# Sliding-window attention and squared-ReLU MLP, two layers on one core: LayerNorm transposes by DMA, and attention logits that arrive already spread over the partitions

## The chip, the cores and the metric

The kernel runs on one core of a Trainium2 chip. The metric is the device time of one execution in microseconds (us), median of several. The 13 executions of the kernel before lie within 0.15% (1329.62 to 1331.54 us).

The engines are called by their names in the profile: PE is TensorE (matrix multiply), PEld its weight loads, DVE is VectorE, ACT is ScalarE, POOL is GpSimd, SP is the engine that issues DMAs. An engine's queue, below, is the list of its instructions in the order in which the compiled program has them.

## The reference, cut to what matters

Two layers of attention and two MLPs, 2048 tokens, width 1024, inner width 3584, bfloat16:

```python
x = x + A(layernorm(x));  x = x + B(layernorm(x))      # twice, same weights

# A: 32 heads of 32; token s looks at s, s-2, ... s-14 (W = 8, dilation 2)
logits = einsum("bhsd,bhswd->bhsw", q, kg) * Dh ** -0.5
attn   = softmax(where(idx >= 0, logits, -1e9));  o = einsum("bhsw,bhswd->bhsd", attn, vg)
return o @ wo
# B
h = relu(x @ w1 + b1) ** 2;  return h @ w2 + b2
```

## The kernel before

A block is 512 tokens; there are four blocks to a layer, so eight in all, numbered 0 to 7. PE's program for block u is, in this order: the query and key projections of block u+1 (128 matmuls of 128x512), the output projection of block u (64, `py<-wt,oT`), the value projection of block u+1 (64, `pq`), the MLP of block u (224 up, `ph`; 224 down, `py<-wt,r2t`). Attention on DVE and LayerNorm on ACT are woven in beside it by a scheduler that estimates when each input is ready.

LayerNorm of a tile of 128 tokens, then eight PE transposes into PSUM and a copy out:

```python
def ln_transpose(self, xt, xnT, tl, dve_stats=False, evac_act=False):
    if dve_stats:   # bn_stats, bn_aggr on DVE; Ln, Exp on ACT; nmr on DVE
        ...
    else:           # two passes of ACT over the tile (sum, then square), then five small ones
        nc.scalar.activation(out=xn[:], in_=xt, func=ACTF.Identity, accum_out=s1[:])
        ...
        nc.scalar.activation(out=xn[:], in_=xt, func=ACTF.Square, bias=nmean[:], scale=1.0, accum_out=s2[:])
        ...
    nc.scalar.activation(out=xn[:], in_=xt, func=ACTF.Identity, bias=nmr[:], scale=rstd[:])
    pt = self.ps_t.tile([128, self.KD, 128], BF, name="pt", tag="pt")
    for kd in range(self.KD):
        nc.tensor.transpose(pt[:, kd, :], xn[:, kd * 128:(kd + 1) * 128], self.ident[:])
    with self.tc.high_priority():
        ...         # copy to xnT on VectorE, in three blocks on ScalarE
```

Attention of a half block (256 tokens, `hb`): for each of eight chunks c, DVE makes the product P of q with eight shifted views of k. In blocks 1 to 7 a tree adds the eight P in fours; PE sums over the channels of a head with small matmuls (`lg`, 32 columns). In block 0 (`STREAM`) there is no tree: PE adds all eight. Softmax follows, with tokens on the partitions; then the probabilities are copied four times (`p4`) and transposed back on PE (`ptp`):

```python
    # prod:  P = q * shifted k;  STREAM: stream_red(d, P) on PE;  else two levels of the tree
    # red:   for w in range(W): for i, Pp in enumerate(d["finals"]):
    nc.tensor.matmul(lg[:, tl2, w, :], Pp[:, w, tl2 * 128:(tl2 + 1) * 128], self.ind[:], ...)
    # sm:    max, subtract, Exp      p4f: sum, reciprocal, p4 = z * l
    # tr:
    nc.tensor.transpose(ptp[:, w, :], p4[:, tl2, w].rearrange("p h r -> p (h r)"), self.ident[:])
    nc.scalar.copy(pb[:, :, tl2 * 128:(tl2 + 1) * 128], ptp[:])
    # av:    pr = pb * shifted v, three adds -> oT
```

## Time and profile before

| | before |
|---|---|
| time, median of 4 | 1330.51 us (1329.84 to 1330.92) |
| span of the profiled execution | 1328.1 us |
| PE / DVE / ACT busy | 97% / 62% / 51% |
| 128x512 matmuls | 5632, starts 216 ns apart |
| distance from one block's MLP to the next, blocks 2 to 6 | 161.1 us |

From the groups of instructions of the kernel before, by shape. Columns: line, engine, operation, output<-inputs, shape, count | busy us, mean ns of one | idle time of the engine in front of them and what ended it:

```profile
L485 PE MATMUL ph<-xnT,wt 128*128 128x512 bf16 x1792 | 395.1, 380 | 0.8 <-DVE xnT L198 0.8
...
L335 DVE TENSOR_TENSOR P<-P 128x2048 bf16<-128x2048 bf16 x84 | 102.3, 1219 | 0.4
...
L193 PE MATMUL pt<-ident,xn 128*128 128x128 bf16 x512 | 41.5, 227 | 29.3 <-ACT xn L190 28.6
...
L398 PE MATMUL ptp<-ident,p 128*128 128x128 bf16 x256 | 17.1, 219 | 0.6 <-DVE p L386 0.5
...
L362 PE MATMUL lg<-ind,P 128*128 128x32 bf16 x448 | 13.7, 177 | 0.7 <-DVE P L335 0.7
...
L349 PE MATMUL lg<-ind,P 128*128 128x32 bf16 x256 | 8.9, 177 | 0.1
```

A PE instruction lasts longer than the distance to the next (380 ns against 216 for `ph`, 227 against 56 for `pt`; they overlap), so costs are counted by the distance of starts: 216 ns for 512 columns, 56 ns for a transpose in a stream of eight between matmuls, 25 ns for a 32-column logit matmul, all at a granted clock of 1.00. The group of LayerNorm transposes (`pt`) also carries PE's largest wait, 28.6 us for `xn` of ACT.

The timeline of PE in block 2 of the kernel before (start us, us, what, count, [idle before it <- what ended it]) shows how those waits lie:

```profile
426.95 9.66 PE L457 MATMUL py<-wt,oT 128*128 128x512 bf16 x44
437.51 0.62 PE L193 MATMUL pt<-ident,xn 128*128 128x128 bf16 x8 [0.90 <-ACT xn L190]
437.97 4.48 PE L457 MATMUL py<-wt,oT 128*128 128x512 bf16 x20
...
443.12 0.62 PE L193 MATMUL pt<-ident,xn 128*128 128x128 bf16 x8 [0.24 <-ACT xn L190]
443.58 5.79 PE L268 MATMUL pq<-xnT,wt 128*128 128x512 bf16 x26
449.55 0.62 PE L193 MATMUL pt<-ident,xn 128*128 128x128 bf16 x8 [0.19 <-ACT xn L190]
```

### The profile page before, as it was taken

What the parts mean: (1) busy time and instruction counts of PE and PEld (TensorE: products, weight loads), DVE (VectorE), ACT (ScalarE), POOL (GpSimd) and SP (SyncE); (2) the same over time, 40 slices, a digit from 0 to 9 for tenths busy, and PEclk for the clock granted to TensorE, in tenths of its full rate; (3) what the DMA queues carried; (4) which work ended last, traced back from release to release, by engine and by line L of the source; (5) the groups of instructions that cost most, each with busy time, mean ns of one, the idle gap of its engine ahead of it and who ended that gap; (6) DMA issues with size and microseconds to landing.
All of it is one profiled execution on the core that took longest, in us unless ns stands there. A gap on an engine that the chain in (4) does not pass through costs nothing.

```text
span 1328.1 us, 17393 instructions
## 1 busy us (share of the span) xinstructions
PE 1292.2 (97%) x7104; PEld 679.8 (51%) x7104; DVE 830.0 (62%) x1170; ACT 681.1 (51%) x1229; POOL 2.9 (0%) x9
## 2 busy tenths in 40 slices
PE   6999999999999999999999999999999999998998
PEld 3665444654446544455445554455544555443443
DVE  4599993394934949268582777719676197926011
ACT  4647826287342964239561494615836166142622
POOL 0000000000000000000000000000000000000000
PEclk9999999999999999999999999999999999999999
DMA  8434544546355554656457464456644564346341
GB/s 214 160 127 158 175 138 151 203 160 203 124 197 185 180 175 143 199 189 207 122 176 233 161 221 151 137 188 211 202 127 163 193 216 137 122 151 225 127 135 56
DMA packets 180847, 223.69 MB, mean 168 GB/s; under 512 B 8608, under 2 KB 143776, under 8 KB 180768
## 3 DMA queue, kind: packets, MB, share of 16 engines
q1 hardware_dynamic: 177168, 222.58, 51.1%
q0 software_dynamic: 3600, 0.01, 0.4%
q8 instruction: 55, 0.90, 0.3%
q14 instruction: 24, 0.20, 0.0%
HBM read 209.98 MB, written 12.58 MB: 168 GB/s over the span
## 4 chain that ended last, share of the span: by engine, by line
PE 73%; DVE 14%; ACT 11%; issue 1%; DMA 0%; SPq 0%; ACTq 0%
PE py L506 29%; PE ph L485 28%; PE pq L268 12%; DVE P L316 5%; DVE P L335 4%; ACT xn L190 3%; ACT xn L181 3%; ACT xn L185 2%; PE pt L193 1%; DVE pr L411 1%; PE py L457 1%; PE ptp L398 1%; DVE xm L459 1%; ACT vT L270 1%; PE lg L362 1%
## 5 line engine op out<-in xcount | busy, mean ns | idle before, releaser
L485 PE MATMUL ph<-xnT,wt 128*128 128x512 bf16 x1792 | 395.1, 380 | 0.8 <-DVE xnT L198 0.8
L506 PE MATMUL py<-wt,r2t 128*128 128x512 bf16 x1792 | 392.6, 379 | 0.0
L268 PE MATMUL pq<-xnT,wt 128*128 128x512 bf16 x1536 | 344.5, 381 | 0.8 <-DVE xnT L198 0.8
L506 PEld LDWEIGHTS <-r2t 128*128 128x128 bf16 x1792 | 174.5, 98 | 207.1 <-ACT r2t L490 0.4
L485 PEld LDWEIGHTS <-wt 128*128 128x128 bf16 x1792 | 174.2, 98 | 206.5 <-issue 2.9
L268 PEld LDWEIGHTS <-wt 128*128 128x128 bf16 x1536 | 216.7, 144 | 107.0 <-issue 3.0
L489 ACT ACTIVATE r<-ph,b1T 128x512 bf16<-128x512 f32 x224 | 152.9, 683 | 98.2 <-PE ph L485 97.2
L411 DVE TENSOR_TENSOR pr<-pb,vT 128x2048 bf16<-128x2048 bf16 x128 | 155.1, 1226 | 44.2 <-ACT pb L399 44.2
L316 DVE TENSOR_TENSOR P<-qT,kT 128x2048 bf16<-128x2048 bf16 x128 | 153.5, 1224 | 36.6 <-ACT qT L270 36.5
L490 ACT ACTIVATE r2t<-r 128x512 bf16<-128x512 bf16 x224 | 140.6, 629 | 5.5
L270 ACT CAST kT<-pq 128x512 bf16<-128x512 f32 x64 | 37.6, 587 | 188.9 <-PE pq L268 188.9
L457 PE MATMUL py<-wt,oT 128*128 128x512 bf16 x512 | 115.1, 383 | 0.0
L335 DVE TENSOR_TENSOR P<-P 128x2048 bf16<-128x2048 bf16 x84 | 102.3, 1219 | 0.4
L412 DVE TENSOR_TENSOR pr<-pr 128x1024 bf16<-128x1024 bf16 x128 | 86.3, 688 | 0.0
L516 DVE TENSOR_TENSOR xo<-py,xm 128x512 bf16<-128x512 f32 x32 | 22.1, 692 | 101.9 <-PE py L506 101.9
L399 ACT COPY pb<-ptp 128x1024 bf16<-128x1024 bf16 x32 | 31.6, 1013 | 104.1 <-PE ptp L398 103.9
L457 PEld LDWEIGHTS <-oT 128*128 128x128 bf16 x512 | 50.0, 99 | 59.1 <-issue 2.0
L512 DVE TENSOR_TENSOR xm<-py,xm 128x512 f32<-128x512 f32 x64 | 44.0, 687 | 52.0 <-PE py L506 52.0
L270 ACT CAST qT<-pq 128x512 bf16<-128x512 f32 x64 | 37.5, 586 | 65.3 <-PE pq L268 65.3
L193 PE MATMUL pt<-ident,xn 128*128 128x128 bf16 x512 | 41.5, 227 | 29.3 <-ACT xn L190 28.6
L521 DVE TENSOR_TENSOR xof<-py,xm 128x512 f32<-128x512 f32 x32 | 22.1, 692 | 76.4 <-PE py L506 56.5
L193 PEld LDWEIGHTS <-xn 128*128 128x128 bf16 x512 | 32.4, 101 | 51.6 <-ACT xn L190 45.7
(61 smaller groups left out, 734.2 us busy)
## 6 DMA issues: line engine op xcount, KB each, us to landing
wt<-in_B_w_dram SPq DMA_DIRECT2D x88, 1024.0 KB, 6.1
wt<-in_A_wqkv_dram SPq DMA_DIRECT2D x48, 1024.0 KB, 6.3
wt<-in_B_w_dram SPq DMA_DIRECT2D x32, 768.0 KB, 4.6
wt<-in_A_wo_dram SPq DMA_DIRECT2D x16, 1024.0 KB, 6.2
xt<-xs SPq DMA_DIRECT2D x32, 512.0 KB, 4.5
xt<-in_A_x_dram SPq DMA_DIRECT2D x32, 256.0 KB, 3.6
xs<-xof SPq DMA_DIRECT2D x32, 256.0 KB, 3.0
out_dram<-xo SPq DMA_DIRECT2D x32, 128.0 KB, 2.0
```

The costliest lines, as they stand in the source:

```text
L193: nc.tensor.transpose(pt[:, kd, :], xn[:, kd * 128:(kd + 1) * 128], self.ident[:])
L268: nc.tensor.matmul(pq[:], fetch(nm)[kd // 4][:, kd % 4, c0:D:8], xnT[:, kd, :], start=(kd == 0), stop=(kd == KD - 1))
L270: nc.scalar.copy(dst[:, c0, off:off + BLK], pq[:])
L316: pi = nc.vector.tensor_tensor(P[:], qT[:, c, None, hb * HB:(hb + 1) * HB].to_broadcast([128, W, HB]), _win_ap(kT[:, c, :], HALO + hb * HB ...
L335: nc.vector.tensor_tensor(other[:], other[:], cur[:], ALU.add)
L411: nc.vector.tensor_tensor(pr[:], pb[:], vwin, ALU.mult)
L412: nc.vector.tensor_tensor(pr[:, 0:4, :], pr[:, 0:4, :], pr[:, 4:8, :], ALU.add)
L457: nc.tensor.matmul(py[:], oT[:, c, tl * 128:(tl + 1) * 128], wos[db][:, c, :], start=(c == 0), stop=(c == NCH - 1))
L485: nc.tensor.matmul(ph[:], wt[:, kd, cc * 128:(cc + 1) * 128], xnT[:, kd, :], start=(kd == 0), stop=(kd == KD - 1))
L489: nc.scalar.activation(out=r[:], in_=ph[:], func=ACTF.Relu, bias=self.b1T[:, f_idx:f_idx + 1], scale=1.0)
L490: nc.scalar.activation(out=r2t[:], in_=r[:], func=ACTF.Square)
L506: nc.tensor.matmul(py[:], r2[kf][:, tl * 128:(tl + 1) * 128], w2s[gi][:, j, :], start=(kf == 0), stop=(kf == KFH - 1))
```

## The change

Its intent: to take work off PE. (1) LayerNorm tiles are transposed by DMA from SBUF to SBUF, except in block 0's first LayerNorm, the last block's second, and the fourth tile of each second LayerNorm. (2) One 128x128 group matrix sums the channels of a head and spreads the result over the head's partitions in one step, so logits come out in the layout in which they are needed; no transposing back, no maximum. (3) The tree on DVE goes all the way, in block 0 too. (4) float16 in attention. The core of the diff:

```diff
-        self.ind = const.tile([128, H], BF, name="ind")
+        self.grp = const.tile([128, H, 4], F16, name="grp")      # 1 where both channels are of one head
+        self.mask01 = const.tile([128, W, HALO], F32, name="mask01")
...
-        xn = self.xp.tile([128, D], BF, name="xn", tag="xn")
+        xn = self.xp.tile([128, D], BF, name="xn", tag="xn", bufs=4)
...
+        if scr is not None:
+            with self.tc.high_priority():
+                nc.sync.dma_start_transpose(xnT[:, tl], xn[:])
+            return
...
-        xnT = self.act.tile([128, self.KD, BLK], BF, name="xnT", tag="xnT")
+        xnT = self.act.tile([128, 4, self.KD, 128], BF, name="xnT", tag="xnT")
...
-                if STREAM: ... stream_red(d, P)
-                while lvl in d["levels"] and lvl < MAXL:
+                while lvl in levels:
                     nc.vector.tensor_tensor(other[:], other[:], cur[:], ALU.add)
...
         def red(hb):
+            for j in range(W // 2):
+                lg = self.ps_lg.tile([128, 2, HB], F32, name="lg", tag="lg")
+                nc.tensor.matmul(lg[:], self.grp[:].rearrange("p h r -> p (h r)"), P[:, 2 * j:2 * j + 2, :], start=True, stop=True)
+                nc.scalar.activation(out=e[:, 2 * j:2 * j + 2, :], in_=lg[:], func=ACTF.Exp, scale=self.scale)
-        def sm / p4f / tr
+        def norm(hb):        # mask, three adds over w, reciprocal, pb = e * ri
...
-            self.ln_transpose(xm[:], xnT, tl, dve_stats=(u == self.n_layers * self.NB - 1), evac_act=(u == 0))
+            last = u == self.n_layers * self.NB - 1
+            self.ln_transpose(xm[:], xnT, tl, dve_stats=last,
+                              scr=None if last or tl == 3 else self.xnd[...])    # only whether it is None counts
```

392 of 512 LayerNorm transposes leave PE for 49 DMA transposes, 120 stay; 256 probability transposes vanish; 704 small logit matmuls become 64 of 512 columns.

## The prediction

> **What bounds it now.** TensorE. The page: PE 97% busy, VectorE 62%, ScalarE 51%, DMA half. There are 5632 matmuls of 128x512; in the trace one starts 216 ns after the other (the timeline has 80 in 17.28 us). [...] That is 1216.5 us of the 1328.1 us span. The other 111.6 us: start to the first projection 17.2; tail 3.6; 512 LayerNorm transposes at 56 ns (28.7); 256 probability transposes at 56 ns (14.3); 704 small logit matmuls at 25 ns (17.6); waits of PE for LayerNorm in the last unit about 7.5; the rest: cold start, and waits of 0.6 to 1.3 us at LayerNorm transposes for xn. One block takes 161.1 us in the steady part (the chain's projection stretches start that far apart).
>
> **What the change does.**
> 1. 392 of 512 LayerNorm transposes become 49 DMA transposes (256 KB each); -22 us on PE, and most of the waits for xn before them, about -6.
> 2. Probability transposes vanish: -14. 704 logit matmuls become 64 of 512 columns: 13.8 against 17.6, -4. All on the critical engine.
> 3. VectorE: the tree gets 28 more full adds (1.14 us apart in the timeline), 112 for 84; 37 xnT copies (0.69 us) go; softmax in the wide layout costs an estimated 6.4 us a half block (f32 adds 2.0; reciprocal of 256, from 549 ns for 64, 2.2; 2048-wide f32 product 2.2) against about 5.5. ScalarE loses the 32 copies of 1013 ns and 12 of 1008, and gets 48 more exps.
>
> In the steady blocks VectorE has room (about 85 of 150 us for attention), so the PE savings count: an estimated 155 to 156 us a block.
>
> **The loss.** In block 0 PE has only projections to do before it needs attention, 320 matmuls. Its logits were streamed on PE without a tree; now VectorE must do 14 tree adds (16 us). In the trace its last attention product of block 0 ends near 114 us and PE finishes the output projection at 120. After, I count from the last q at 48: products and adds to 72, normalise 78, first half 97, normalise and four residual adds 106, second half 124; PE, ready near 90, waits about 25 us in the output projection and ends it near 131, 11 us later than now. The rest after that: 1208.2 us now, an estimated 1169 then.
>
> **DMA transposes.** A 256 KB load lands in 3.6 us here. [...] The third tile's has 7 to 8 us before the MLP's first matmul. Mostly hidden.
>
> **Prediction:** 1302 us (-2.1%), 8 in 10 between 1284 and 1325. Faster by over 2%: 0.50; within 2%: 0.43; slower by over 2%: 0.07.
>
> **What would show it.** Starts of the chain's projection stretches 155 to 156 us apart. PE waiting on VectorE's oT about 25 us in the first output projection, and nowhere else. Adds x112, no ptp group, lg x64 at 216 ns. [...] little PE wait on DMA.
>
> **What would make it wrong.** Transposes that land in 10 us or more, or hold up weight loads behind them on the one queue: a stall in every block. Strided xnT reads over 216 ns. A smaller wait in block 0 (then about 1285).

The sum: 11 us more in block 0 and 39 us less in the rest, 1302 us. Its 2.0 and 2.2 us for f32 adds and product lie near what DVE takes for f32 in the kernel before, 1218 ns for 1024 columns, 687 for 512 and 428 for 256. What it calls cold start is a slower pace at the start of that trace: eight transposes take 1.03 us at 10.4 us and 0.62 us at 35.9 us, at a granted clock of 1.00 both times; the cause isn't shown.

## More of the kernel before

From the page of the kernel before, the span, part 1 (busy us, share of the span, instructions) and part 2's line for ACT (tenths busy in 40 slices):

```profile
span 1328.1 us, 17393 instructions
PE 1292.2 (97%) x7104; PEld 679.8 (51%) x7104; DVE 830.0 (62%) x1170; ACT 681.1 (51%) x1229; POOL 2.9 (0%) x9
...
ACT  4647826287342964239561494615836166142622
```

PE is the engine to relieve.

## The result, and the profile after

| | before | after | predicted |
|---|---|---|---|
| time, median | 1330.53 us (13 runs) | 1307.4 us (8 runs) | 1302, 1284 to 1325 |
| ratio | | 0.9827 [0.9817, 0.9836] | 0.979 |
| block 0's output projection ends | 119.9 us | 124.6 us | 131 us |
| the rest of the span | 1208.2 us | 1181.0 us | 1169 us |
| distance from one block's MLP to the next, blocks 2 to 6 | 161.1 us | 155.7 to 157.8 us | 155 to 156 us |

Ratios are the mean time of one kernel's runs over that of the other's of the same rounds, so not quite the ratio of the quoted medians. Executions over 1.5% slower than the fastest of the same kernel are left out of the means.

From the page of the changed kernel, the same lines:

```profile
span 1305.6 us, 14886 instructions
PE 1255.2 (96%) x5816; PEld 636.3 (49%) x5816; DVE 856.6 (66%) x1143; ACT 655.8 (50%) x1233; POOL 3.4 (0%) x9
...
ACT  4734934279142892239731495415934167142622
```

The groups of the changed kernel that answer to those above, in the same columns:

```profile
L323 DVE TENSOR_TENSOR P<-P 128x2048 f16<-128x2048 f16 x112 | 136.2, 1220 | 1.1
...
L397 PE MATMUL py<-wt,oT 128*128 128x512 bf16 x512 | 118.1, 391 | 11.4 <-DVE oT L364 11.4
...
L348 DVE RECIPROCAL ri<-dn 128x256 f32<-128x256 f32 x16 | 28.0, 1749 | 0.2
...
L335 PE MATMUL lg<-P,grp 128*128 128x512 f16 x64 | 17.3, 390 | 2.5 <-DVE P L323 2.5
...
L196 PE MATMUL pt<-ident,xn 128*128 128x128 bf16 x120 | 11.6, 254 | 29.7 <-ACT xn L189 29.6
```

The counts are the ones that the diff promises: 112 tree adds of the same 1220 ns, 64 logit matmuls, no `ptp` group, 120 `pt`. But look at the last column of the last line. There are 392 fewer transposes on PE, and PE still waits 29.6 us at them for `xn` of ACT, where it waited 28.6 us before. The work went, the wait stayed. (Without the start of the kernel and the last block, where the change takes nothing from the waits, the idle time at `pt` is 11.3 us before and 12.4 us after.)

The DMA transposes themselves are quick. From the changed kernel's list of DMA issues (what, queue, count, median us from issue to landing):

```profile
xnT<-xn SPq DMA_TRANSPOSE x49, 3.3
```

They land in 2.7 to 6.5 us, and one, 256 KB, holds SP 1.23 us in the median (1.63 at most). Packets under 512 B rose from 8608 to 60352 with the 49 transposes, (60352 - 8608) / 49 = 1056 for each.

Two places of the changed kernel's PE timeline show the cost and the wait. Block 0, its output projection, which begins at 93.2 us:

```profile
93.21 1.67 PE L397 MATMUL py<-wt,oT 128*128 128x512 bf16 x7
96.01 5.57 PE L397 MATMUL py<-wt,oT 128*128 128x512 bf16 x25 [1.13 <-DVE oT L364]
108.96 3.60 PE L397 MATMUL py<-wt,oT 128*128 128x512 bf16 x8 [7.38 <-DVE oT L364]
113.52 3.59 PE L397 MATMUL py<-wt,oT 128*128 128x512 bf16 x8 [0.96 <-DVE oT L364]
...
122.64 1.90 PE L397 MATMUL py<-wt,oT 128*128 128x512 bf16 x8 [0.96 <-DVE oT L364]
124.58 11.81 PE L273 MATMUL pq<-xnT,wt 128*128 128x512 bf16 x54
```

PE waits here for DVE. From 93.0 to 124.6 us DVE is busy 31.60 of 31.60 us, so only less work on DVE in front of it, or another order of that work, can shorten it. The 64 matmuls would take 13.8 us at 216 ns; they take 31.4 us: 11.4 us of waits, and 20 us for the matmuls, which run at a granted clock of 0.73 in the mean of this stretch. (The clock is 1.00 up to 104.6 us, 0.50 from there, 3 us into the wait of 7.4 us, to 121.7 us, and 1.00 after that; the next pair of `oT` chunks comes 4.6 us after the one before, and the eight matmuls for a pair take 3.6 us even so, so here the slow clock hides behind DVE.)

Block 2, the stretch that stands for the steady blocks:

```profile
424.39 13.98 PE L397 MATMUL py<-wt,oT 128*128 128x512 bf16 x64
438.20 11.82 PE L273 MATMUL pq<-xnT,wt 128*128 128x512 bf16 x54
451.93 0.62 PE L196 MATMUL pt<-ident,xn 128*128 128x128 bf16 x8 [1.91 <-ACT xn L189]
452.39 2.33 PE L273 MATMUL pq<-xnT,wt 128*128 128x512 bf16 x10
454.56 1.89 PE L427 MATMUL ph<-xnT,wt 128*128 128x512 bf16 x8
```

Before, four tiles of transposes lay here, each behind a wait of 0.1 to 0.9 us. Now one tile is left, the fourth, and it alone waits 1.9 us. The output projection runs without a break (64 matmuls in one group). Counted from its start, PE gets to the fourth tile at 25.6 us (26.0 before), but ACT ends that tile's `xn` only at 27.5 us (26.1 before).

How busy is ACT there? The table of stretches gives, for a stretch, its length, the busy us (and instructions) of PE, PEld, DVE, ACT and POOL, the granted clock, the DMA share and GB/s. Taken from the first LayerNorm pass of block 2's output projection to a place 2 to 6 us into the MLP's first down-projection (cut where that begins, ACT's shares below are the same within 4 points); before, then after:

```profile
432.60:490.50 57.90, 56.45 (x352) 30.07 (x351) 39.57 (x45) 52.10 (x98) 0.00 (x0) 1.00 0.55 181
```

```profile
430.00:486.60 56.60, 54.55 (x259) 27.56 (x258) 53.34 (x68) 56.03 (x116) 0.00 (x0) 1.00 0.78 220
```

ACT is busy 52.10 of 57.90 us before (90%), and 56.03 of 56.60 us after (99%). In the rest of the same period it is busy 26.68 of 94.30 us. So ACT, 50% busy over the span, has almost no slack for a third of this block, which stands for the steady ones, and that is the third in which PE needs LayerNorm from it. The busiest engine differs within one period: in this stretch it is ACT (56.03 us against PE's 54.55), in the rest PE (94.30 of 94.30 us).

This gives the theory that the experiments test: **PE's removed work pays in full, but PE's waits are set by ACT's load between the output projection and the middle of the MLP's first half, and removing PE work doesn't shorten them.** Rivals: the wait belongs to the place of the fourth tile's transposes in PE's order; it belongs to the fourth tile being on PE at all; or the loss is all in block 0, in the DVE tree.

### The profile page after: what moved, and what is told of

It is laid out like the page before. It is cut to its first block, busy times and chain, and to the rows that moved or that the text cites. A ratio compares the mean times of both kernels' runs of the same rounds, so it can differ in the third digit from the quotient of the medians.

```text
span 1305.6 us, 14886 instructions
## 1 busy us (share of the span) xinstructions
PE 1255.2 (96%) x5816; PEld 636.3 (49%) x5816; DVE 856.6 (66%) x1143; ACT 655.8 (50%) x1233; POOL 3.4 (0%) x9
## 2 busy tenths in 40 slices
DMA packets 232582, 236.39 MB, mean 181 GB/s; under 512 B 60352, under 2 KB 195520, under 8 KB 232512
## 4 chain that ended last, share of the span: by engine, by line
PE 60%; ACT 19%; DVE 16%; issue 2%; DMA 2%; SPq 0%; ACTq 0%
PE py L448 29%; PE ph L427 21%; PE pq L273 9%; DVE P L314 6%; DVE P L323 4%; ACT xn L184 4%; ACT xn L180 3%; ACT r L431 3%; ACT r2t L432 3%; ACT xn L189 3%; DVE xm L399 1%; DVE pr L361 1%; ACT vT L275 1%; DMA xt<-in_A_x_dram 1%; DVE xm L405 1%
## 5 line engine op out<-in xcount | busy, mean ns | idle before, releaser
L273 PE MATMUL pq<-xnT,wt 128*128 128x512 bf16 x1536 | 339.2, 382 | 0.8 <-DVE xnT L201 0.8
L427 PEld LDWEIGHTS <-wt 128*128 128x128 bf16 x1792 | 175.9, 98 | 213.8 <-issue 4.3
L273 PEld LDWEIGHTS <-wt 128*128 128x128 bf16 x1536 | 220.2, 144 | 114.9 <-issue 5.0
L314 DVE TENSOR_TENSOR P<-qT,kT 128x2048 f16<-128x2048 f16 x128 | 154.0, 1224 | 30.1 <-ACT qT L275 30.0
L361 DVE TENSOR_TENSOR pr<-pb,vT 128x2048 f16<-128x2048 f16 x128 | 153.0, 1224 | 0.3
L323 DVE TENSOR_TENSOR P<-P 128x2048 f16<-128x2048 f16 x112 | 136.2, 1220 | 1.1
L275 ACT CAST kT<-pq 128x512 f16<-128x512 f32 x64 | 37.5, 587 | 191.7 <-PE pq L273 188.3
L397 PE MATMUL py<-wt,oT 128*128 128x512 bf16 x512 | 118.1, 391 | 11.4 <-DVE oT L364 11.4
L362 DVE TENSOR_TENSOR pr<-pr 128x1024 f16<-128x1024 f16 x128 | 84.3, 685 | 0.0
L275 ACT CAST qT<-pq 128x512 f16<-128x512 f32 x64 | 37.4, 584 | 64.5 <-PE pq L273 64.5
L336 ACT ACTIVATE e<-lg 128x512 f32<-128x512 f32 x64 | 34.7, 606 | 50.7 <-PE lg L335 49.5
L180 ACT ACTIVATE xn<-xm 128x1024 bf16<-128x1024 f32 x28 | 29.3, 1048 | 50.9 <-DVE xm L399 50.9
```

Source lines behind the costliest of these rows:

```text
L273: nc.tensor.matmul(pq[:], fetch(nm)[kd // 4][:, kd % 4, c0:D:8], xnT[:, :, kd, :], start=(kd == 0), stop=(kd == KD - 1))
L275: nc.scalar.copy(dst[:, c0, off:off + BLK], pq[:])
L314: pi = nc.vector.tensor_tensor(cur[:], qT[:, c, None, hb * HB:(hb + 1) * HB].to_broadcast([128, W, HB]), _win_ap(kT[:, c, :], HALO + hb * ...
L323: nc.vector.tensor_tensor(other[:], other[:], cur[:], ALU.add)
L361: nc.vector.tensor_tensor(pr[:], pb[:], vwin, ALU.mult)
L362: nc.vector.tensor_tensor(pr[:, 0:4, :], pr[:, 0:4, :], pr[:, 4:8, :], ALU.add)
```

## The experiments

Eleven further kernels ran, one of them twice (e7, e7b); all gave correct results. Each was compared with the kernel before on the same chip; "us" is the median of the fast runs. The expectations speak of theories by letter; the numbers beside them tell what each would have meant. "Waits per block" below are worked out from the trace: the distance from each PE matmul's start to the next, less 216, 56 or 25 ns for the kind, summed from the start of block 2's MLP to that of block 6's where it exceeds 60 ns, divided by four. Some traces lack 50 to 65 matmul records; a gap of a whole 216 ns, which a missing record or a granted clock of 0.50 leaves (eight matmuls take 3.60 us at it in block 0 of the changed kernel, 1.90 us at 1.00), isn't counted. "Period" is the distance from the start of one block's MLP to the next one's; the range has all six, but where the first is given apart.

| kernel | us | ratio to before [95%] | period, us | waits per block, us |
|---|---|---|---|---|
| before | 1330.5 | 1 | 161.1; first 163.0 | 2.1 |
| after | 1307.4 | 0.9827 [0.9817, 0.9836] | 155.7 to 157.8; first 159.4 | 2.7 |
| e1_pe_ln | 1325.4 | 0.9961 [0.9946, 0.9976] | 159.4 to 160.3 | 2.1 |
| e2_dma_ln_only | 1327.0 | 0.9984 [0.9966, 1.0002] | 158.3 to 160.3; first 165.9 | 3.4 |
| e3_stream0 | 1307.9 | 0.9835 [0.9819, 0.9851] | 156.5 to 160.6 | 2.9 |
| e4_stats3 | 1320.9 | 0.9920 [0.9905, 0.9935] | 156.2 to 159.0 | 3.0 |
| e7_tl3_dma | 1305.2 | 0.9815 [0.9799, 0.9832] | (one profile, e7b) 154.1 to 160.5 | 2.6 |
| e8_bf16 | 1306.8 | 0.9825 [0.9810, 0.9839] | like after | 2.6 |
| e9b_late_stats | 1322.3 | 0.9932 [0.9916, 0.9947] | 156.5 to 159.7 | 3.5 |
| e10_all | 1315.6 | 0.9886 [0.9871, 0.9901] | 156.6 to 158.4 | 3.2 |
| e11_mid | 1304.3 | 0.9810 [0.9794, 0.9825] | 154.6 to 157.7 | 2.6 |
| e14_mid_sa | 1293.1 | 0.9720 [0.9707, 0.9734] | 154.1 to 156.9 | 0.1 |
| e15_mid_sa_stream | 1290.9 | 0.9704 [0.9691, 0.9717] | 154.1 to 157.3 | 0.1 |

### e1_pe_ln: the attention half of the change alone

All LayerNorm transposes back on PE, the rest as in the changed kernel:

```diff
-                              scr=None if u == 0 else self.xnd[...])
+                              scr=None)
...
-                              scr=None if last or tl == 3 else self.xnd[...])
+                              scr=None)
```

> The changed kernel with all LayerNorm transposes back on TensorE; the attention rewrite stays. Theory A (a TensorE transpose costs its 56 ns on the engine that bounds, and the wait of 2.3 us a block for the last LayerNorm tile comes from ScalarE's chain and has nothing to do with DMA): 392 transposes come back, of which 64 fall into block 0's wait, so about +18 us: 1326 us, and the waits for xn are still 2 to 3 us a block. Rival B (the DMA transposes cause the wait for LayerNorm, by latency or by holding up the queue): the waits shrink to well under 1 us a block, about -12 us against A: 1314 us or less.

Measured: 1325.4 us, on theory A's 1326. Five us less than before; block 0's MLP starts 6.7 us later (141.9 against 135.2 us), the first period is 2.7 us shorter, and each later one 0.8 to 1.7 us. Waits per block are what they were before, 2.1 us, with no DMA transpose at all, so rival B is out. ACT's share of the stretch is 98% here.

### e2_dma_ln_only: the DMA transposes alone

The kernel before, with the DMA transposes in the same places as the changed kernel, the same layout of `xnT`, and four `xn` buffers:

```diff
+        if dma:
+            with self.tc.high_priority():
+                nc.sync.dma_start_transpose(xnT[:, tl], xn[:])
+            return
...
-            self.ln_transpose(xt, xnT, tl, dve_stats=(u == 0), evac_act=(1 <= u <= 2))
+            self.ln_transpose(xt, xnT, tl, dve_stats=(u == 0), dma=(u > 0))
...
+                              dma=(u < last and tl < 3))           # second LayerNorm (written short)
```

> The kernel before with one part of the change alone: LayerNorm transposes by DMA as in the changed kernel, the old attention (streamed block 0, two-level tree, probability transposes) stays. Theory A: 392 transposes of 56 ns leave TensorE, about -22 us, the wait for the last tile stays: 1306 to 1310 us, so nearly all of the whole change's 23 us. The attention rewrite would then be worth about nothing in sum (about -15 us in the steady blocks, against a longer wait in block 0). Rival (the attention rewrite carries the gain, DMA transposes are given back in waits): 1318 us or more.

Measured: 1327.0 us, where 1306 to 1310 was expected. This is the largest miss. 56 transposes a block went (7 tiles of 8, 3.1 us at 56 ns), yet the waits rose from 2.1 to 3.4 us a block, so a steady period is only about 2 us shorter (161.1 - 3.14 + 1.27 = 159.2; 158.3 to 160.3 measured). The stretch in question, of this kernel:

```profile
435.90:495.50 59.60, 57.37 (x339) 30.19 (x339) 39.20 (x44) 57.64 (x116) 0.00 (x0) 1.00 0.76 223
```

ACT is busy 57.64 of 59.60 us: here ACT keeps its copies of `ptp` besides the LayerNorm, and its delay shows at the fourth tile, and later at the MLP's `r2t`. In addition the first period grew, 165.9 us against 163.0. The trace shows where: PE waits 2.3 and 0.5 us at `ptp` (166.7 and 167.9 us) for DVE's `p`, behind a DVE that had itself waited 2.4 us for ACT's exponentials (162.7 us), and 3.4 us at `pt` (299.7 us) for ACT's `xn`; after the waits at `ptp` PE is slower too: four 128x512 matmuls from 168.7 us take 1.91 us, where four take 1.03 us at a granted clock of 1.00 (e11). ACT is busy 12.94 of the 13.00 us from 155 to 168 us, so this is ACT's load once more. The four `xn` buffers weren't tried alone.

So -5.3 (e1, ratio 0.9961) and -3.6 us alone (e2, by the medians; its interval reaches 1, so it isn't clear of noise), but -23 us together. The two halves don't add. By the traces the together is better by about 4 us before block 0's MLP, 4 in the first period, 5 in the next five and 1 in the tail. A reason, argued and not tested: each half leaves ACT the load that the other removes or spreads, or leaves PE work that hides the waits.

### e7_tl3_dma and e7b_tl3_dma: the fourth tile by DMA too

```diff
-                              scr=None if last or tl == 3 else self.xnd[...])
+                              scr=None if last else self.xnd[...])
```

> The changed kernel with the fourth tile's LayerNorm transpose on DMA as well (seven more). Theory A: the tile is ready at the same time from ScalarE, then needs 1.2 us of issue and 3.3 us to land instead of 0.5 us on TensorE and a copy of 0.7 us, so the wait moves from before the transposes to before the MLP's first matmul and grows: 0.5 to 1.5 us a block, 1311 to 1318 us. Rival (latency of the DMA is hidden, the last tile needs no exception): 1304 us, by the 56 transposes saved.

Measured: 1305.2 us in three runs (1304.4 to 1308.3), the same as the changed kernel; 1311 to 1318 was expected. A fourth execution took 1904.4 us at a granted clock of 0.656, whose cause no run tells (with it the median is 1306.8), and the profile fell there.

> The fourth tile's transpose by DMA once more, for a profile at full clock (the one of the earlier run fell in a stretch at a granted clock of 0.656). Its time was that of the changed kernel within the interval. If the wait only moved: about 2 to 2.5 us a block in front of the MLP's first matmul, none at transposes, and the period 156 to 157 us.

Measured: 1307.9 us in the one run (state unknown, clock 0.986). PE's timeline in block 2:

```profile
440.76 13.98 PE L273 MATMUL pq<-xnT,wt 128*128 128x512 bf16 x64
457.44 1.89 PE L427 MATMUL ph<-xnT,wt 128*128 128x512 bf16 x8 [2.27 <-DMA xnT<-xn]
```

The value projection now runs unbroken, and the wait has moved to the MLP's first matmul: 2.3 us for the DMA transpose of the last tile. That rules out the rival that the fourth tile loses because it is on PE. ACT ends `xn` 27.5 us after the output projection's start, as in the changed kernel. That alone would be no wait here: it is 0.7 us before PE is free. The 2.3 us come of ACT's late `xn` and the 3.0 us to landing together.

### e8_bf16: bfloat16 in place of float16

```diff
-F16 = mybir.dt.float16
+F16 = mybir.dt.bfloat16
```

> The changed kernel with bfloat16 in the attention tensors in place of float16. If the data type does not matter for time (both have 2 bytes): 1307 us, VectorE products still 1.22 us. The error against the reference should be larger. Rival: the float16 products or the float16 logit matmul run at another pace, then the mean of these groups differs by over 5%.

Measured: 1306.8 us, periods as in the changed kernel, correct. float16 neither costs nor gains time; the tree adds take 1218 ns here against 1220 in the changed kernel. The record has no error figure, so the expectation of a larger error stays unchecked.

### e3_stream0: block 0's logits streamed on PE again

```diff
+                if u == 0:       # no tree: PE sums the eight chunks into four open groups
+                    for j in range(W // 2):
+                        nc.tensor.matmul(lgs[j][:], grp, cur[:, 2 * j:2 * j + 2, :],
+                                         start=(c == 0), stop=(c == NCH - 1))
+                    continue
...
-            e = self.att.tile([128, W, HB], F32, name="e", tag="e")
+            e = self.att.tile([128, W, HB], F32, name="e", tag="e", bufs=2)
```

> The changed kernel, but block 0 adds its eight products up on TensorE (64 logit matmuls for 8) with no tree on VectorE, as the kernel before did in its own layout; a second buffer for the exponentials. Theory A (the wait of TensorE in the first output projection, about 17 us in all, is VectorE's queue of work, of which the 14 tree adds are 16 us): VectorE ends block 0's attention near 113 us instead of 122.7, TensorE has 12 us more to do but in time that it waited: the first output projection ends near 115 us instead of 124.5, total about -9 us: 1298 us. Rival (the wait has another cause, or TensorE's added 12 us count in full): 1307 to 1319 us.

Measured: 1307.9 us, the same as the changed kernel. Block 0's output projection ends at 121.2 us instead of 124.6, and its MLP starts 2.6 us earlier (136.8 against 139.4). An arithmetic slip of the expectation: with PE at work until 105.0 us and 64 matmuls to come (13.8 us), 119 us was the least possible. The gain is gone later: the next period is 160.6 us against 159.4, and those after it up to 158.4. The second `e` buffer is a confound. So the tree in block 0 costs 2.6 to 3.4 us there, and while ACT limits the blocks after it, taking it back is worth nothing.

### e4_stats3: the fourth tile's statistics on DVE

```diff
-            self.ln_transpose(xm[:], xnT, tl, dve_stats=last,
+            self.ln_transpose(xm[:], xnT, tl, dve_stats=last or tl == 3,
```

> The changed kernel with the statistics of the fourth tile's LayerNorm taken on VectorE (bn_stats) instead of two passes on ScalarE. Theory C (the wait for the last tile depends on how long ScalarE's chain is): ready about 2.5 us earlier, the wait of 2.3 us a block vanishes, about -14 us: 1294 us. Theory D (it depends on where the schedule puts the eight transposes in TensorE's queue: here they move up from behind 54 to behind 38 matmuls of the projection in most blocks, 3.5 us earlier, because the scheduler also believes in the earlier xn): a wait of 1.5 to 3 us a block remains: 1304 to 1309 us.

Measured: 1320.9 us, 13.5 us worse than the changed kernel. PE, in block 0:

```profile
124.36 13.97 PE L273 MATMUL pq<-xnT,wt 128*128 128x512 bf16 x64
148.18 1.03 PE L196 MATMUL pt<-ident,xn 128*128 128x128 bf16 x8 [9.85 <-ACT xn L189]
```

In block 0 DVE is the engine with the backlog. The two statistics instructions stood in its queue behind attention and ran at 141.95 and 143.67 us; PE waited 9.9 us, and block 0's MLP began at 151.1 us, 11.7 us later. In the steady blocks the waits stayed at 3.0 us and split between the transposes (7.3 us in four blocks) and the MLP's `r2t` (4.7 us). In block 2 `xn` is finished 3.7 us sooner (23.8 us after the output projection's start, against 27.5), but the compiled order has the transposes sooner too, behind 38 matmuls of the value projection and not 54, and PE waits 1.7 us. That is what theory D said of the steady blocks; the loss in block 0 it didn't foresee. Moving one tile's statistics away from ACT isn't enough, and in block 0 it goes to the wrong engine.

### e9b_late_stats: the same, with the transposes after the value projection

```diff
+        if late:
+            return finish            # the eight PE transposes and the copy, to be called later
...
+            if nm == "wv" and c0 == NCH - 1 and u > 0:
+                self.late_pt()
```

> As the run before (statistics of the fourth tile on VectorE), and the eight transposes are put later in the program, so that they stand behind 56 or 64 matmuls of the projection. Theory D: xn is there when TensorE reaches them, the wait is under 0.5 us a block (at most 1 us before the MLP where they stand at the very end): about -13 us, 1294 us. If a wait of 2 us stays at the transposes or reappears in front of the MLP's first matmul for another reason (a DMA transpose of tiles 0 to 2 not landed): 1304 to 1308 us.

Measured: 1322.3 us. Block 0 lost as in e4 (MLP at 150.5 us). In block 2 the wait moved again. PE, then DVE, of the same stretch:

```profile
461.08 0.61 PE L197 MATMUL pt<-ident,xn 128*128 128x128 bf16 x8
461.53 1.90 PE L276 MATMUL pq<-xnT,wt 128*128 128x512 bf16 x8
465.23 1.89 PE L430 MATMUL ph<-xnT,wt 128*128 128x512 bf16 x8 [1.80 <-ACT nmr L188]
```

```profile
461.03 1.22 DVE L326 TENSOR_TENSOR P<-P 128x2048 f16<-128x2048 f16 x1
462.17 2.36 DVE L317 TENSOR_TENSOR P<-qT,kT 128x2048 f16<-128x2048 f16 x2
464.44 0.68 DVE L199 COPY xnT<-pt 128x1024 bf16<-128x1024 bf16 x1
```

The transposes no longer wait, but their copy out of PSUM stands behind three wide attention instructions on DVE and ends at 465.1 us; the MLP's first matmul starts 0.1 us after it. The profile names "ACT nmr" as what ended that wait, but the fourth tile's `nmr` had been done at 457.7 us, before the transposes ran: the name printed isn't what ended this wait, it was the copy. So this wait, 2.0 us a block, ends on DVE in every block (0.1 us after the copy); another 1.5 us a block stands at ACT's `r2t`.

### e10_all: e3 and e9b together

> Both mends together: block 0 streamed, fourth tile's statistics on VectorE and its transposes late. If the two waits are independent the gains add: -9 and -13 us, 1285 us (3.4% below the kernel before). If they share a cause or one gives back what the other takes: 1294 us or more.

Measured: 1315.6 us, with block 0's MLP at 147.1 us and periods of 156.6 to 158.4 us. Streaming relieves DVE in block 0 and gives back 6.8 us of what e9b lost (by the medians; 3.4 us of it before block 0's MLP), but against the changed kernel nothing was gained in the steady blocks.

### e11_mid: the transposes in the middle of the value projection, DVE statistics not in block 0

```diff
-            if nm == "wv" and c0 == NCH - 1 and u > 0:
+            if nm == "wv" and c0 == 6 and u > 0:
...
-            self.late_pt = self.ln_transpose(xm[:], xnT, tl, dve_stats=last or tl == 3, ...)
+            self.late_pt = self.ln_transpose(xm[:], xnT, tl, dve_stats=last or (tl == 3 and u > 0), ...)
```

> The changed kernel with the fourth tile's statistics on VectorE in blocks 1 to 7 only (not in block 0, where VectorE is behind with attention), and its transposes behind 48 of the 64 value-projection matmuls. Read from the two runs before: xn is ready about 23.8 us after the output projection begins, TensorE comes to the transposes at 24.2 us, and the copy out of PSUM has 3.4 us until the MLP needs it. Theory E (the 2 us a block are a race of three places: ScalarE's chain, the place of the transposes in TensorE's queue, and VectorE's queue in front of the copy): the wait before the MLP falls below 0.5 us a block, the period from 156.5 to about 154.8 us, the total by about 11 us: 1296 us; block 0's MLP starts at 139 us as in the changed kernel. Rival (there is a floor of about 2 us a block whose place alone moves, as in the two runs before): 1305 to 1309 us.

Measured: 1304.3 us. This is the run that kills the rival of place. PE hardly waits at the fourth tile in the steady blocks, or before the MLP (0.5 us in four blocks). It waits 2.6 us a block all the same (9.9 us in four blocks at `r2t`), in the middle of the MLP:

```profile
478.52 3.19 PE L451 MATMUL py<-wt,r2t 128*128 128x512 bf16 x14
482.93 0.39 PE L451 MATMUL py<-wt,r2t 128*128 128x512 bf16 x1 [1.22 <-ACT r2t L435]
484.17 2.12 PE L451 MATMUL py<-wt,r2t 128*128 128x512 bf16 x9 [0.85 <-ACT r2t L435]
```

`r2t` is the square of the squared ReLU, made by ACT. ACT in that stretch is at 54.19 of 56.40 us (96%). Its queue is behind, and PE pays the delay where it first needs what ACT has not made yet.

### e14_mid_sa: less LayerNorm on ACT

e11, and the statistics of the first LayerNorm also on DVE, in all blocks but block 1 (before, in block 0 alone):

```diff
-            self.ln_transpose(xt, xnT, tl, dve_stats=(u == 0),
+            self.ln_transpose(xt, xnT, tl, dve_stats=(u != 1),
```

> As the run before, and the first LayerNorm's statistics (tiles of blocks 2 to 7) on VectorE too, 24 tiles. Theory F (the waits of up to 1.2 us for r2t at the first down-projection matmuls are ScalarE's backlog, which two LayerNorm passes a tile add to): these waits vanish, 0.3 to 0.6 us a block: 2 to 4 us under the run before. Rival (VectorE now holds the chain up, as it did in block 0 with the statistics there): equal or slower.

Measured: 1293.1 us, 11.2 us below e11 by one flag; 2 to 4 us was expected, too little, since e11's `r2t` wait alone was 2.5 us a block. The stretch, of e11 and of this kernel:

```profile
427.60:484.00 56.40, 54.50 (x258) 27.55 (x256) 54.63 (x72) 54.19 (x110) 0.00 (x0) 1.00 0.75 221
```

```profile
427.10:482.00 54.90, 54.90 (x262) 28.01 (x261) 54.38 (x75) 42.98 (x80) 0.00 (x0) 1.00 0.79 228
```

ACT fell from 54.19 to 42.98 us (96% to 78%), and PE from 54.50 busy of 56.40 us to 54.90 of 54.90: no idle. The place where e11 waited runs through in this kernel:

```profile
478.09 5.13 PE L451 MATMUL py<-wt,r2t 128*128 128x512 bf16 x23
```

Waits are 0.12 us a block, and four periods in a row are 154.1 us. PE's own work in a block of the changed kernel is 704 x 0.216 + 8 x 0.216 + 8 x 0.056 = 154.2 us, so nothing is left to take but work. DVE took the statistics without harm: 54.38 us busy in the stretch against e11's 54.63. That also answers the rival that DVE, just as full in this stretch, makes PE wait: at 99% of it (54.38 of 54.90 us) PE doesn't wait at all.

### e15_mid_sa_stream: with block 0 streamed

e14 and e3's streaming.

> As the run before, with block 0 streamed. In the earlier run streaming alone started block 0's MLP 2.6 us earlier and gave it back later. If the blocks after it are no longer held by ScalarE, the 2.6 us stay: 2 to 3 us under the run before. If not, no difference.

Measured: 1290.9 us, the fastest kernel: 39.6 us below before and 16.5 us below the changed kernel. Block 0's MLP starts 3.6 us earlier than in e14 (135.0 against 138.6), and 2.2 us of that reach the end by the medians (the runs of the two overlap, 1289.2 to 1292.7 against 1292.3 to 1293.9, so the size is not firm). The same streaming gained nothing in e3, where ACT set the pace of the later blocks.

## Why the prediction was right, and where it was wrong

**Right: PE bounds the kernel, and its removed work pays.** A steady period by PE's own work: before, 704 x 0.216 + 64 x 0.056 (LayerNorm) + 32 x 0.056 (`ptp`) + 64 x 0.025 (logits) = 159.0 us, and 2.1 us of waits, which makes 161.1 (161.1 measured). After, 154.2 and 2.7 us of waits, which makes 156.9 (157.0 measured in the mean of the same four periods). The DMA transposes landed in 3.3 us in the median, 2.7 to 6.5, and matmuls that read `xnT` in the new layout still start 216 ns apart (120 `ph` in 26.06 us in block 2).

**Right in kind, mis-sized: the loss in block 0.** The step "and ends it near 131, 11 us later than now" was 124.6 us, 4.7 us later. PE was ready at 93.2 us ("near 90") and DVE was the limit, as said. But "waits about 25 us" was 17.6 us over the matmuls' own 13.8: 11.4 us of waits and some 6 us of slower clock. The count let the second half's matmuls begin only when its attention had ended. In fact PE takes each pair of chunks of `oT` as it comes, and after the last pair only 8 matmuls are left (the last line of 8 at 122.64 us). The reciprocal of 256 columns, f32, was 1.75 us, not 2.2, which is four times the 549 ns of 64: (1749 - 549) / 192 = 6.25 ns for each further column. e3 confirms the size from the other side: streaming ends the projection 3.4 us earlier.

**Wrong: "and most of the waits for xn before them, about -6".** They were 28.6 us and became 29.6 (11.3 and 12.4 without the start and the last block); with them failed "PE waiting on VectorE's oT [...] and nowhere else" and the 1169 us for the rest of the span, which was 1181.0. Summed by the rule for waits from the end of block 0's output projection to the last matmul, PE's own work fell from 1181.5 to 1150.6 us, and its gaps, those of a half clock with them, rose from 22.8 to 26.8 us: +4.1 where -6 was predicted, which is 10 of the 12 us that were missing. I took a wait to belong to the instruction that it is printed at. In the steady blocks it belonged to ACT's load: ACT was already 90% busy in that stretch before, and became 99%, with 116 of its instructions in a stretch that held 98 before.

The chain of runs shows it. The wait turned up at the MLP's first matmul with the last transpose by DMA (e7b), was split with the statistics moved (e4), stood behind a copy on DVE and at `r2t` (e9b), then at `r2t` nearly alone (e11), 2.6 to 3.5 us a block each time. Its last link was not always ACT: the landing in e7b, the copy in e9b. It went only when ACT's load in the stretch fell to 78% (e14), by one flag over e11. What is not shown: the flag of e14 on the changed kernel without e11's placement wasn't run, so how much each of the two needs the other is open.

**The sum.** Predicted +11 in block 0 and -39 in the rest; measured +4.7 and -27.2, which is the span's -22.5. Two errors of about 6 and 12 us in opposite directions left 1307.4 us against 1302, inside the range. That the number came so close is in part luck: a right answer with two mis-sized terms, one of them with a wrong sign in it. The gain is 1.7%, under the 2% to whose passing the prediction gave 0.50.

**Still open.** Why the two halves of the change gain more together than alone. Whether block 0 has a better split than all tree or all streaming. Whether PE could do block 1's value projection during block 0's wait (it needs a second buffer for v; not tried).

## What to carry to other kernels

Don't subtract a wait together with the work that it is printed at: ask how busy the engine it waits for is in that stretch, because a producer without slack (here ACT, at 96 to 99% of the stretch) makes the consumer wait somewhere, and with work taken from the consumer the waits can grow (here from 2.1 to 2.7 us a block). Read that share from a stretch of one period, not from the span: 50% over the span was 99% where it mattered. When a wait only moves as you reorder the consumer, take work from the producer (here, with e11's order kept, ACT fell from 96% to 78% of the stretch and the waits from 2.6 to 0.1 us a block); and a gain early in the kernel (block 0's streaming) can be absorbed by a later limit (all of it in e3).
